# Softmax sums spread and returned by small DMAs, with one stream shuffle in place of two DVE transposes, in a sliding-window attention and GEGLU kernel

## Chip, cores and metric

The kernel runs on one NeuronCore of a Trainium2 chip. The metric is the device time of one execution in microseconds. PE is TensorE (PEld its weight loads), DVE VectorE, ACT ScalarE, POOL GpSimd, and SP the engine whose queue issues most of the DMAs. Each engine works through its own instructions in order.

## What is computed

The input x is one sequence of 2048 rows and 448 columns in bf16. The output is x plus causal attention of 16 heads (28 columns each, a window of 256 keys) plus a GEGLU feed-forward part of 1792 columns, both on the layer-normed x.

```python
qkv = (x @ wqkv) ...                                   # q, k, v: 16 heads of 28
scores = einsum("bhqd,bhkd->bhqk", q, k) * (Dh ** -0.5)
mask = (idx[:, None] - idx[None, :] >= 0) & (idx[:, None] - idx[None, :] < 256)
p = softmax(where(mask, scores, -1e9), axis=-1)
A = einsum("bhqk,bhkd->bhqd", p, v) ... @ wo
B = (gelu(x @ w_gate) * (x @ w_up)) @ w_down
return x + A(layernorm(x)) + B(layernorm(x))
```

The kernel takes the exponential without subtracting a maximum, and carries a column of ones behind the 28 columns of v (line 137), so that the product of p and v also gives the sum of p, the softmax sum, as a 29th row of each head. What the change touches is how that sum is inverted and multiplied into the product.

## The kernel before, in words

The 2048 queries are four blocks of 512 (`qb` 0 to 3, loop at line 613). Each block has an attention part (`attention`, line 445) and a feed-forward part (`gated`, line 338); the down projection of a block (`gen_down`, which also multiplies by wo) and the projections of the next (`gen_proj`) or, in the last block, `gen_up`, are cut into pieces and fed between the attention steps of the following block, by costs in ns (`Feed`, `share`, `drain`). All of this happens while the program is built; on the chip every engine has a fixed order.

The 16 heads are four groups `g` of four. A group's four heads lie in the four quarters of the partitions, 32 each: in quarter j, rows 0 to 27 are the head's columns and row 28 is its softmax sum. Blocks 1 to 3 have ten steps (`steps_of`, numbered `i` from 0). In step i, in this order:

- the masks of step i-1, three DVE products of 64-key tiles (`apply_masks`, line 432);
- `inverse()` for a group whose product is ready (line 500);
- at steps 4, 6 and 9, `pv(g)` of groups 0, 1 and 2: the products of p and v go to two PSUM banks (`ov`, line 476, for the two halves of keys), ACT copies the first to `oh` (line 482), DVE adds the second and writes `oc` (line 483);
- the score matmuls into `sc` (line 509), four PSUM banks and only one such tile, and ACT's exponential to `p_sb` (line 513);
- `scale_o()`: POOL multiplies `oc` by the inverses `rb` into `oN` (line 465), which `gen_down` reads in the next block;
- pieces of the fed work: po (lines 296, 301), pq and pk (line 218), ue (line 218), each with an eviction: `res` by DVE and its store by SP (lines 306, 307), `qT` by ACT, `kT` by DVE (266, 267), `hT` by DVE (335).

Group 3 has its `pv(3)` in `rest()` (line 539), which runs inside the first feed-forward pair (`f = 0`), followed by its inverse in `hook(0)`. Block 0 has twelve steps, its masks are done by POOL, and it has no `oh`.

`inverse()` (line 450) takes the sum out of row 28 of each quarter. DVE transposes `oc` in 32x32 blocks to `l1` (line 454), copies the sums, now 16 a partition, to `l_all` (455), takes the reciprocal (457), and transposes a broadcast of it back (459), so that `rb` holds each query's inverse in all 32 rows of its quarter. `oc` and `rb` have one buffer each; `l1` and `oh` share one.

PSUM has two banks of the tag `m`, one of `o` and one of `d`, and the four of the scores. `ov` takes both `m` banks (group 3: one `m` and one other), and so do, in turn, the fed pq, pk, pv and ue. So the matmuls that next need an `m` bank wait until `oh` (first bank) and `oc` (second bank) have read it. After the attention the four score banks become two `gt` tiles; the first up-projections `u` of `f = 0` come ahead of the first `gt`, and the first of them takes an `m` bank.

At the end DVE compares all the sums in `l_all` with two limits; a general path runs if one is outside, which does not happen with these inputs.

Of the kernel before, what the change touches and what calls it, by code (L numbers as in the profile page):

```python
# [9 lines left out]
ALU = mybir.AluOpType  # L10
AX = mybir.AxisListType
bf16 = mybir.dt.bfloat16
f32 = mybir.dt.float32
i32 = mybir.dt.int32

S, D, H, Dh, F = 2048, 448, 16, 28, 1792
P = 128
NT = S // P
NF = F // P
QB, NB = 512, 4  # L20
# [55 lines left out]
def kernel(  # L76
# [11 lines left out]
    nc = tc.nc  # L88
# [3 lines left out]
    work = fast.enter_context(tc.tile_pool(name="work", bufs=3))  # L92
# [82 lines left out]
    l_all = const.tile([P, NB * 4, 16], f32, name="l_all")  # L175
# [269 lines left out]
    def attention(qb, feeds, aux, plan):  # L445
        oN = blk.tile([P, 4, QB], bf16, name="oN")
        oNs[qb] = oN
        parts, copied, later, fresh = {}, [], [], []

        def inverse():  # L450
            while copied:
                g, oc = copied.pop(0)
                l1 = work.tile([P, 16, 32], f32, name="l1", tag="l1", bufs=1)
                nc.vector.transpose(out=l1[:, :, :].rearrange("p a b -> p (a b)"), in_=oc[:, :])
                nc.vector.tensor_copy(out=l_all[:, 4 * qb + g, :], in_=l1[:, :, Dh])
                ri = work.tile([P, 16], f32, name="ri")
                nc.vector.reciprocal(out=ri[:, :], in_=l_all[:, 4 * qb + g, :])
                rb = work.tile([P, 16, 32], f32, name="rb", bufs=1)
                nc.vector.transpose(out=rb[:, :, :], in_=ri[:, :].unsqueeze(2).to_broadcast([P, 16, 32]))  # L459
                later.append((g, oc, rb))  # L460

        def scale_o():
            while later:
                g, oc, rb = later.pop(0)
                nc.gpsimd.tensor_tensor(out=oN[:, g, :], in0=oc[:, :], in1=rb[:, :, :].rearrange("p a b -> p (a b)"), op=ALU.mult)  # L465

        def pv(g):

            tags = ("o",) if not qb else ("m", "m" if g < 3 else down_tag[0])
            ov = [psum.tile([P, QB], f32, name="ov", tag=tag, bufs=2 if tag == "m" else 1) for tag in tags]  # L470
            todo = parts.pop(g)
            for n, (half, kt, q0, nq, col, p_sb) in enumerate(todo):
                k0 = 64 * half if half else 0
                r = slice(k0, k0 + (P if half is None else 64))
                for j in range(4):
                    nc.tensor.matmul(ov[half or 0][32 * j:32 * j + 32, q0:q0 + nq], lhsT=v_sb[r, kt, 4 * g + j, :],  # L476
                                     rhs=p_sb[r, j, col:col + nq], start=n == (half or 0), stop=n + len(tags) >= len(todo),
                                     tile_position=(k0, 32 * j), skip_group_check=True)
            oc = work.tile([P, QB], f32, name="oc", bufs=1)
            if qb:  # L480
                oh = work.tile([P, QB], f32, name="oh", tag="l1", bufs=1)
                nc.scalar.copy(out=oh[:, :], in_=ov[0][:, :])  # L482
                nc.vector.tensor_tensor(out=oc[:, :], in0=oh[:, :], in1=ov[1][:, :], op=ALU.add)  # L483
            else:
                nc.vector.tensor_copy(out=oc[:, :], in_=ov[0][:, :])
            copied.append((g, oc))

        if qb:
            feeds[0].run()
        steps = list(steps_of(qb))  # L490
        pvs = {4: 0, 6: 1, 9: 2} if qb else {4: 0, 7: 1, 10: 2}
        for i, (scores, ncol, edges) in enumerate(steps):
            while (qb, scores[-1][0]) not in done:
                feeds[0].run()
            for fd in feeds:
                if fd.held:
                    fd.run()
            while fresh:
                apply_masks(*fresh.pop(0))
            inverse()  # L500
            if i in pvs:
                pv(pvs[i])
            ss = phase[0].pool.tile([P, 4, QB], f32, name="sc", tag="s")
            p_sb = work.tile([P, 4, QB], bf16, name="p_sb", bufs=5)
            for g, half, kt, q0, nq, col in scores:
                k0, nk = (64 * half, 64) if half is not None else (0, P)
                for j in range(4):
                    r = slice(32 * j, 32 * j + 32)
                    nc.tensor.matmul(ss[k0:k0 + nk, j, col:col + nq], lhsT=kT[r, g, kt * P + k0:kt * P + k0 + nk],  # L509
                                     rhs=qT[r, g, qb * QB + q0:qb * QB + q0 + nq], start=True, stop=True,  # L510
                                     tile_position=(32 * j, k0), skip_group_check=True)
                parts.setdefault(g, []).append((half, kt, q0, nq, col, p_sb))
            nc.scalar.activation(out=p_sb[:, :, 0:ncol], in_=ss[:, :, 0:ncol], func=ACT.Exp, scale=SCALE)  # L513
            if qb:
                fresh.append((p_sb, edges))
            else:
                for m in edges:
                    masked(p_sb, *m)
            scale_o()
            left = len(steps) - i  # L520
            if left == 1:
                drain(feeds)
            elif not qb:
                share(feeds + [Feed()], 1e12, 0)
            else:
                to = plan.get(i, 0)
                whole = sum(f.left for f in feeds) + STEP * left + PV * sum(j > i for j in pvs)
                ahead = STEP + PV * (i + 1 in pvs) + (360 if to > 1000 else 0)
                late = 400 if i == 0 else 0
                want = (whole - late) / (left + 0.2) + late - ahead - to  # L530
                if i in pvs:
                    had = feeds[0].left
                    share(feeds[:1], min(1100, want), 0)
                    want -= had - feeds[0].left
                share(feeds, want, to)
            if aux:
                aux.pop(0)()

        def rest():
            while fresh:  # L540
                apply_masks(*fresh.pop(0))
            after()
            pv(3)
        def after():
            inverse()
            scale_o()
        return rest, after


# [63 lines left out]
    for qb in range(NB):  # L613
        early = ()
        aux, plan = [], {}
        if qb < 2:
            aux = [lambda: rstd(6, 2), lambda: (norm(6), norm(7), loads()), lambda: None] * (1 - qb) + [lambda t=t: stat(t) for t in range(8, 12)] * (1 - qb) + [lambda: rstd(4 * qb + 8, 4)]
        if qb == 0:
            new_hT(0)
            early = (2, 8)  # L620
            feeds = [Feed((v23, 360), (gen_qk(0, (1, 2, 3)), 3 * QK1), (gen_proj(1), PROJ), (gen_up(0, early), UP1 * len(early)))]
            feeds[0].held = True
        else:
            ring[0] = ("m",)
            tags = "dodo" if last_tag[0] == "o" else "odod"
            feeds = [Feed((gen_down(qb - 1, tags), DOWN))]
            if qb < 3:
                feeds.append(Feed((gen_proj(qb + 1), PROJ)))
                plan = {0: 1140, 1: 1140, 2: 1300, 4: 1300, 6: 1300, 7: 1300}
            else:  # L630
                new_hT(3)
                early = (2, 4, 6, 8, 10)
                feeds.append(Feed((gen_up(3, early), UP1 * len(early))))
                plan = {0: 1300, 2: 1300, 4: 1300, 6: 1300, 7: 1300}
        if qb:
            score_pool(1)
        rest, after = attention(qb, feeds, aux, plan)
        nc.scalar.preload_act_table(ACT.Gelu_apprx_tanh)
        score_pool(2)
        if qb not in hTs:  # L640
            new_hT(qb)

        def hook(f):
            if f == 0:
                after()
            elif f >= 4 and qb < 2:
                t = 4 * qb + 4 + f // 2
                if f < 12:
                    norm(t + 2)
                    dma_transp(t + 2)  # L650
                    if qb == 0:
                        stat(t + 6)

        gated(qb, early, rest, hook)
        if qb < NB - 1:
            nc.scalar.preload_act_table_set("natural_log_exp_and_others")


    g1 = work.tile([P, 512], f32, name="g1", tag="l1", bufs=1)
    g2 = work.tile([P, 512], f32, name="g2", tag="rb", bufs=1)  # L660
    okc = const.tile([P, 1], f32, name="okc")
    okb = const.tile([P, 1], bf16, name="okb")
    one = const.tile([P, 1], bf16, name="one")
# [131 lines left out]
```

## Time and profile before

| | before |
|---|---|
| median of 3 runs | 235.08 us (234.16 to 235.28) |
| the profiled execution's own time | 235.08 us |
| its span in the profile | 233.3 us |
| PE busy | 216.8 us, 93% |
| DVE busy | 157.1 us, 67% |
| ACT busy | 133.4 us, 57% |
| POOL busy | 43.3 us, 19% |
| mean granted PE clock | 0.986 |

The span is what lies between the first and last instruction of the profile; 1.8 us of the execution's time lie around it. A group line gives the source line, engine and operation, output and input, count, busy time and mean of one, and the idle time of the engine ahead of it with its releaser. The chain of waits is followed back from the last instruction; it is 82% PE and 10% DVE.

### The profile page before, as it was taken

What the parts mean: (1) busy time and instruction counts of PE and PEld (TensorE: products, weight loads), DVE (VectorE), ACT (ScalarE), POOL (GpSimd) and SP (SyncE); (2) the same over time, 40 slices, a digit from 0 to 9 for tenths busy, and PEclk for the clock granted to TensorE, in tenths of its full rate; (3) what the DMA queues carried; (4) which work ended last, traced back from release to release, by engine and by line L of the source; (5) the groups of instructions that cost most, each with busy time, mean ns of one, the idle gap of its engine ahead of it and who ended that gap; (6) DMA issues with size and microseconds to landing.
All of it is one profiled execution on the core that took longest, in us unless ns stands there. A gap on an engine that the chain in (4) does not pass through costs nothing.

```text
span 233.3 us, 5303 instructions
## 1 busy us (share of the span) xinstructions
PE 216.8 (93%) x2237; PEld 97.2 (42%) x2262; DVE 157.1 (67%) x359; ACT 133.4 (57%) x129; POOL 43.3 (19%) x63
## 2 busy tenths in 40 slices
PE   6789999999999799999999799999999889999990
PEld 2433333344444344444444345444444425444470
DVE  5896877769666795755575886754456877695310
ACT  3578898435878674523778686323867737454000
POOL 8524777220000220210000220220000202220000
PEclk9999999999999999999999999999999979999997
DMA  6917999312100000012100001000000000000011
GB/s 222 301 32 78 302 288 254 125 22 49 22 22 3 20 17 25 4 22 48 22 0 22 24 3 37 5 0 0 3 21 3 22 0 22 20 3 0 21 43 27
DMA packets 15686, 12.58 MB, mean 54 GB/s; under 512 B 7401, under 2 KB 14633, under 8 KB 15657
## 3 DMA queue, kind: packets, MB, share of 16 engines
q1 hardware_dynamic: 15112, 11.38, 18.5%
q10 hardware_dynamic: 544, 0.80, 1.0%
q8 instruction: 19, 0.31, 0.6%
q14 instruction: 11, 0.08, 0.1%
HBM read 8.77 MB, written 1.84 MB: 45 GB/s over the span
## 4 chain that ended last, share of the span: by engine, by line
PE 82%; DVE 10%; DMA 3%; issue 2%; ACT 1%; SPq 0%
PE po L301 17%; PE gt L218 16%; PE u L218 12%; PE gt L223 5%; PE sc L509 5%; PE po L296 5%; PE ue L218 4%; PE pk L218 4%; PE ov L476 4%; PE pv L218 4%; PE pq L218 3%; DVE p_sb L432 3%; DMA wv<-in_A_wqkv_dram 3%; PE pq L223 2%; PE ue L223 1%
## 5 line engine op out<-in xcount | busy, mean ns | idle before, releaser
L513 ACT ACTIVATE p_sb<-sc 128x2048 bf16<-128x2048 f32 (+2 forms) x42 | 73.8, 1758 | 13.6 <-PE sc L509 12.6
L301 PE MATMUL po<-wd,hT 128*128 128x448 bf16 (+1 forms) x238 | 50.2, 343 | 0.0
L465 POOL TENSOR_TENSOR oN<-oc,rb 128x512 bf16<-128x512 f32 x16 | 21.2, 1323 | 150.8 <-DVE rb L459 150.8
L376 ACT ACTIVATE ge<-gt 128x1024 bf16<-128x1024 f32 x28 | 28.7, 1025 | 35.4 <-PE u L223 22.2
L218 PE MATMUL gt<-xnT,wg 128*128 128x512 bf16 x162 | 39.3, 380 | 0.8 <-issue 0.8
L380 DVE TENSOR_TENSOR hT<-ge,u 128x512 bf16<-128x512 bf16 x42 | 26.9, 682 | 17.1 <-ACT ge L376 16.9
L218 PE MATMUL u<-xnT,wu 128*128 128x512 bf16 x120 | 30.2, 379 | 0.3
L432 DVE TENSOR_TENSOR p_sb<-p_sb,masks 128x256 bf16<-128x256 bf16 (+1 forms) x90 | 28.7, 375 | 1.8 <-ACT p_sb L513 1.8
L301 PEld LDWEIGHTS <-hT 128*128 128x128 bf16 x238 | 21.6, 98 | 18.6 <-issue 2.2
L218 PEld LDWEIGHTS <-wu 128*128 128x128 bf16 x168 | 16.3, 99 | 21.9 <-issue 4.2
L218 PEld LDWEIGHTS <-wg 128*128 128x128 bf16 x168 | 15.1, 98 | 21.5 <-issue 5.2
L306 DVE TENSOR_TENSOR res<-po,x_sb 128x448 bf16<-128x448 f32 (+1 forms) x17 | 10.0, 590 | 15.9 <-PE po L301 15.9
L509 PE MATMUL sc<-qT,kT 32*64 32x320 bf16 (+7 forms) x640 | 16.9, 263 | 0.4 <-ACT p_sb L513 0.3
L442 POOL TENSOR_SCALAR_AFFINE_SELECT p_sb<-p_sb 128x512 bf16<-128x512 bf16 (+1 forms) x20 | 14.2, 727 | 13.4 <-ACT p_sb L513 13.4
L296 PE MATMUL po<-wo,oN 128*128 128x448 bf16 (+1 forms) x68 | 16.3, 343 | 0.0
L267 DVE CAST kT<-pk 128x512 bf16<-128x512 f32 (+1 forms) x17 | 10.9, 644 | 7.9 <-PE pk L223 7.9
L218 PE MATMUL pk<-xnT,wkp 128*128 128x512 bf16 (+1 forms) x51 | 13.1, 366 | 3.2 <-DVE oc L483 3.1
L482 ACT COPY oh<-ov 128x512 f32<-128x512 f32 x12 | 7.0, 586 | 15.1 <-PE ov L476 13.0
L266 ACT CAST qT<-pq 128x512 bf16<-128x512 f32 (+1 forms) x17 | 9.5, 559 | 9.9 <-PE pk L223 9.9
L335 DVE CAST hT<-ue 128x512 bf16<-128x512 f32 x14 | 9.0, 687 | 8.2 <-PE ue L223 8.2
L218 PE MATMUL ue<-xnT,wu 128*128 128x512 bf16 x38 | 11.7, 420 | 2.2 <-DVE oc L483 1.8
L223 PE MATMUL gt<-xnT,wgu 64*128 64x512 bf16 x49 | 13.6, 379 | 0.0
(70 smaller groups left out, 228.6 us busy)
## 6 DMA issues: line engine op xcount, KB each, us to landing
out_dram<-res SPq DMA_DIRECT2D x15, 112.0 KB, 1.7
wd<-in_B_w_down_dram SPq DMA_DIRECT2D x1, 1568.0 KB, 12.0
wu<-in_B_w_up_dram SPq DMA_DIRECT2D x1, 1344.0 KB
wg<-in_B_w_gate_dram SPq DMA_DIRECT2D x1, 1344.0 KB, 13.6
x_sb<-in_A_x_dram SPq DMA_DIRECT2D x1, 896.0 KB, 7.1
wraw<-in_A_wqkv_dram ACTq DMA_DIRECT2D x1, 672.0 KB, 5.4
x_sb<-in_A_x_dram SPq DMA_DIRECT2D x1, 448.0 KB, 4.7
wo<-in_A_wo_dram SPq DMA_DIRECT2D x4, 98.0 KB
```

What stands on the lines that cost most here:

```text
L218: nc.tensor.matmul(ps, lhsT=lhs(c), rhs=rhs(c), start=start and c == 0, stop=stop and c == 2, skip_group_check=True)
L223: nc.tensor.matmul(ps, lhsT=lhs[p0:p0 + 64], rhs=rhs[p0:p0 + 64], start=start, stop=stop, tile_position=(p0, 0), skip_group_check=True)
L267: nc.vector.tensor_copy(out=kT[:, g, ts], in_=pk[:, 0:n])
L296: nc.tensor.matmul(po[:, 0:w], lhsT=oN[:, g, cs], rhs=wo[:, g, lo:up], start=(g == 0), stop=False, skip_group_check=True)
L301: nc.tensor.matmul(po[:, 0:w], lhsT=hT[:, f, cs], rhs=wd[:, f, lo:up], start=False, stop=(f == NF - 1), skip_group_check=True)
L376: nc.scalar.activation(out=ge[:, :, :], in_=pr["gt"][:, :, :], func=ACT.Gelu_apprx_tanh)
L380: nc.vector.tensor_tensor(out=hT[:, f + i, :], in0=ge[:, i, :], in1=u[:, :], op=ALU.mult)
L432: nc.vector.tensor_tensor(out=reg, in0=reg, in1=m, op=ALU.mult)
L442: nc.gpsimd.affine_select(out=reg, in_=reg, pattern=mid + [[1 if diag else -1, min(w, P)]], compare_op=ALU.is_ge, fill=0.0, base=0 if diag ...
L465: nc.gpsimd.tensor_tensor(out=oN[:, g, :], in0=oc[:, :], in1=rb[:, :, :].rearrange("p a b -> p (a b)"), op=ALU.mult)
L509: nc.tensor.matmul(ss[k0:k0 + nk, j, col:col + nq], lhsT=kT[r, g, kt * P + k0:kt * P + k0 + nk], rhs=qT[r, g, qb * QB + q0:qb * QB + q0 + ...
L513: nc.scalar.activation(out=p_sb[:, :, 0:ncol], in_=ss[:, :, 0:ncol], func=ACT.Exp, scale=SCALE)
```

## The change

In blocks 1 to 3 `inverse()` is replaced by three functions. `spread` issues four DMAs from SP right after `oc` is written: each takes one quarter's sum row (512 values in one partition) and writes it as 16 values into each of the 32 partitions of the quarter in `l_all`. `back` takes the reciprocal on DVE and issues four DMAs that write the inverses back as one row of `oc`, row 29 of each quarter, which is not otherwise used. `spread_rows` is one DVE stream shuffle that copies row 29 of each quarter to all 32 rows, giving `rb`. `back` runs in steps 5 and 7 (groups 0 and 1, behind the exponential), in `rest()` (group 2, ahead of `pv(3)`) and in `hook(2)` (group 3); `spread_rows` runs ahead of `pv` in steps 7 and 9, in `hook(0)` and in `hook(4)`.

The buffers change too: `oc` alternates between two (`wa`, `wb`), and `oh` and the shuffled `rb` share one (`wc`). Block 0 keeps the two transposes, one group at a time. The DVE masks are the same in both, and in both they come first in each step.

```diff
-        def inverse():
-            while copied:
-                g, oc = copied.pop(0)
-                l1 = work.tile([P, 16, 32], f32, name="l1", tag="l1", bufs=1)
-                nc.vector.transpose(out=l1[:, :, :].rearrange("p a b -> p (a b)"), in_=oc[:, :])
-                nc.vector.tensor_copy(out=l_all[:, 4 * qb + g, :], in_=l1[:, :, Dh])
-                ri = work.tile([P, 16], f32, name="ri")
-                nc.vector.reciprocal(out=ri[:, :], in_=l_all[:, 4 * qb + g, :])
-                rb = work.tile([P, 16, 32], f32, name="rb", bufs=1)
-                nc.vector.transpose(out=rb[:, :, :], in_=ri[:, :].unsqueeze(2).to_broadcast([P, 16, 32]))
-                later.append((g, oc, rb))
+        def inverse(g, oc):
...
+        def spread(g, oc):
+            for j in range(4):
+                nc.sync.dma_start(out=l_all[32 * j:32 * j + 32, 4 * qb + g, :],
+                                  in_=oc[32 * j + Dh:32 * j + Dh + 1, :].rearrange("p (a b) -> p a b", b=16))
+        def back():
+            g, oc = copied[0]
+            ri = work.tile([P, 16], f32, name="ri")
+            nc.vector.reciprocal(out=ri[:, :], in_=l_all[:, 4 * qb + g, :])
+            for j in range(4):
+                nc.sync.dma_start(out=oc[32 * j + Dh + 1:32 * j + Dh + 2, :].rearrange("p (a b) -> p a b", b=16),
+                                  in_=ri[32 * j:32 * j + 32, :])
+        def spread_rows():
+            g, oc = copied.pop(0)
+            rb = work.tile([P, QB], f32, name="rb", tag="wc", bufs=1)
+            nc.vector.stream_shuffle(out=rb[:, :], in_=oc[:, :], mask=[Dh + 1] * 32)
+            later.append((g, oc, rb))
...
-            oc = work.tile([P, QB], f32, name="oc", bufs=1)
+            oc = work.tile([P, QB], f32, name="oc", tag="wb" if qb and g % 2 else "wa", bufs=1)
             if qb:
-                oh = work.tile([P, QB], f32, name="oh", tag="l1", bufs=1)
+                oh = work.tile([P, QB], f32, name="oh", tag="wc", bufs=1)
                 nc.scalar.copy(out=oh[:, :], in_=ov[0][:, :])
                 nc.vector.tensor_tensor(out=oc[:, :], in0=oh[:, :], in1=ov[1][:, :], op=ALU.add)
...
             copied.append((g, oc))
+            if qb:
+                spread(g, oc)
...
             while fresh:
                 apply_masks(*fresh.pop(0))
-            inverse()
+            if not qb and copied:
+                inverse(*copied.pop(0))
+            if qb and i in (7, 9):
+                spread_rows()
             if i in pvs:
                 pv(pvs[i])
...
             scale_o()
+            if qb and i in (5, 7):
+                back()
...
         def rest():
             while fresh:
                 apply_masks(*fresh.pop(0))
-            after()
+            if qb:
+                back()
             pv(3)
-        def after():
-            inverse()
-            scale_o()
+        def after(f):
+            if f == 0:
+                if qb:
+                    spread_rows()
+                else:
+                    inverse(*copied.pop(0))
+                scale_o()
+            elif qb and f == 2:
+                back()
+            elif qb and f == 4:
+                spread_rows()
+                scale_o()
...
         def hook(f):
-            if f == 0:
-                after()
-            elif f >= 4 and qb < 2:
+            after(f)
+            if f >= 4 and qb < 2:
```

More of the change, by code (lines that the diff above doesn't have):

```diff
@@ L448, in attention @@
         parts, copied, later, fresh = {}, [], [], []
-        def inverse():
-            while copied:
-                g, oc = copied.pop(0)
-                l1 = work.tile([P, 16, 32], f32, name="l1", tag="l1", bufs=1)
-                nc.vector.transpose(out=l1[:, :, :].rearrange("p a b -> p (a b)"), in_=oc[:, :])
-                nc.vector.tensor_copy(out=l_all[:, 4 * qb + g, :], in_=l1[:, :, Dh])
-                ri = work.tile([P, 16], f32, name="ri")
-                nc.vector.reciprocal(out=ri[:, :], in_=l_all[:, 4 * qb + g, :])
-                rb = work.tile([P, 16, 32], f32, name="rb", bufs=1)
-                nc.vector.transpose(out=rb[:, :, :], in_=ri[:, :].unsqueeze(2).to_broadcast([P, 16, 32]))
-                later.append((g, oc, rb))
+        def inverse(g, oc):
+            l1 = work.tile([P, 16, 32], f32, name="l1", tag="wc", bufs=1)
+            nc.vector.transpose(out=l1[:, :, :].rearrange("p a b -> p (a b)"), in_=oc[:, :])
+            nc.vector.tensor_copy(out=l_all[:, g, :], in_=l1[:, :, Dh])
+            ri = work.tile([P, 16], f32, name="ri")
+            nc.vector.reciprocal(out=ri[:, :], in_=l_all[:, g, :])
+            rb = work.tile([P, QB], f32, name="rb", tag="wb", bufs=1)
+            nc.vector.transpose(out=rb[:, :].rearrange("p (a b) -> p a b", b=32), in_=ri[:, :].unsqueeze(2).to_broadcast([P, 16, 32]))
+            later.append((g, oc, rb))
[5 more added lines that the diff above has]
+            g, oc = copied[0]
+            ri = work.tile([P, 16], f32, name="ri")
+            nc.vector.reciprocal(out=ri[:, :], in_=l_all[:, 4 * qb + g, :])
[6 more added lines that the diff above has]
+            nc.vector.stream_shuffle(out=rb[:, :], in_=oc[:, :], mask=[Dh + 1] * 32)
+            later.append((g, oc, rb))
         def scale_o():
@@ L464, in scale_o @@
                 g, oc, rb = later.pop(0)
-                nc.gpsimd.tensor_tensor(out=oN[:, g, :], in0=oc[:, :], in1=rb[:, :, :].rearrange("p a b -> p (a b)"), op=ALU.mult)
+                nc.gpsimd.tensor_tensor(out=oN[:, g, :], in0=oc[:, :], in1=rb[:, :], op=ALU.mult)
         def pv(g):
@@ L656 @@
             nc.scalar.preload_act_table_set("natural_log_exp_and_others")
-    g1 = work.tile([P, 512], f32, name="g1", tag="l1", bufs=1)
-    g2 = work.tile([P, 512], f32, name="g2", tag="rb", bufs=1)
+    g1 = work.tile([P, 512], f32, name="g1", tag="wc", bufs=1)
+    g2 = work.tile([P, 512], f32, name="g2", tag="wb", bufs=1)
     okc = const.tile([P, 1], f32, name="okc")
```

## The prediction

> **What bounds the kernel now.** I read the page first, then PE's waits, then the timeline around each of them, then the same stretch of every engine one step later.
>
> ```profile
> PE 216.8 (93%) x2237; PEld 97.2 (42%) x2262; DVE 157.1 (67%) x359; ACT 133.4 (57%) x129; POOL 43.3 (19%) x63
> ```
>
> PE is the bound: 16.5 us of the span are not PE's, and the DMA loads at the start and the last store take most of that. DVE at 67% is no bound on average, so work taken from it is worth only what PE waits for DVE. PE's waits say where that is:
>
> ```profile
> PE pk L218 <- DVE oc L483: 3.1, 2, 1.6
> PE ue L218 <- DVE oc L483: 1.8, 1, 1.8
> PE sc L509 <- ACT p_sb L513: 0.3, 1, 0.3
> ```
>
> Three waits, 1.53, 1.62 and 1.84 us, one in each of blocks 1 to 3: 4.99 us in all. PE wants an `m` bank that `oc` of group 1 has not yet read. No other wait in mid-kernel is over 0.3 us. The timeline of block 1 at this place:
>
> ```profile
> 73.32 0.69 DVE L267 CAST kT<-pk 128x512 bf16<-128x512 f32 x1 [1.51 <-PE pk L223]
> 73.93 0.82 DVE L432 TENSOR_TENSOR p_sb<-p_sb,masks 128x256 bf16<-128x256 bf16 x3
> 74.66 0.71 DVE L454 STREAM_TRANSPOSE l<-oc 128x512 f32<-128x512 f32 x1
> 75.41 0.18 DVE L455 COPY l_all<-l 128x16 f32<-128x16 f32 x1
> 75.62 0.25 DVE L457 RECIPROCAL ri<-l_all 128x16 f32<-128x16 f32 x1
> 75.90 0.71 DVE L459 STREAM_TRANSPOSE rb<-ri 128x512 f32<-128x512 f32 x1
> 76.54 0.58 DVE L306 TENSOR_TENSOR res<-po,x_sb 128x448 bf16<-128x448 f32 x1
> 76.69 1.27 POOL L465 TENSOR_TENSOR oN<-oc,rb 128x512 bf16<-128x512 f32 x1 [28.44 <-DVE rb L459]
> 77.05 1.60 DVE L432 TENSOR_TENSOR p_sb<-p_sb,masks 128x256 bf16<-128x256 bf16 x3
> 78.57 0.67 DVE L483 TENSOR_TENSOR oc<-oh,ov 128x512 f32<-128x512 f32 x1
> 79.30 0.81 PE L218 MATMUL pk<-xnT,wkp 128*128 128x512 bf16 x3 [1.53 <-DVE oc L483]
> ```
>
> See two things: the inverse of group 0 (74.66 to 76.61) stands ahead of everything `oc` waits for, and the three masks behind it take 1.60 us while POOL scales, against 0.82 just before. PE had been ready since 77.77. The second place is step 9, where nothing waits today:
>
> ```profile
> 85.54 0.75 PE L476 MATMUL ov<-p_sb,v_sb 64*32 64x320 bf16 x48
> 86.37 0.59 ACT L482 COPY oh<-ov 128x512 f32<-128x512 f32 x1 [0.71 <-ACT p_sb L513]
> 86.86 1.88 ACT L513 ACTIVATE p_sb<-sc 128x2048 bf16<-128x2048 f32 x1
> 89.62 1.46 PE L218 MATMUL u<-xnT,wu 128*128 128x512 bf16 x5
> 90.92 1.46 PE L218 MATMUL gt<-xnT,wg 128*128 128x512 bf16 x6
> ```
>
> `u` takes the bank that `oh` reads, `gt` the banks that the exponential reads. Counted from the start P of `pv(2)`, they start at P+4.08 and P+5.38; today `oh` ends at P+1.42 and the exponential at P+3.20.
>
> **What the skill says.** "VectorE: DVE Perf Modes", the perf-mode tier table: a stream shuffle has only a one-element-per-cycle program, and one-rate operations fit (N+151)/0.96 ns. For 512 elements that is an estimate of 0.69 us; the two transposes here took 0.705 and 0.711, which agrees. "SBUF — State Buffer", Who interferes with whom: a DVE instruction with two SBUF inputs and a GpSimd instruction that reads SBUF block each other. The 1.60 against 0.82 us agrees. "DMA: Bandwidth & Descriptors", Anatomy of one DMA: a DMA has a fixed cost of about 2.0 us whatever its size, most of it the receipt of the last write, heaviest for HBM. No SBUF-to-SBUF copy is in this trace; stores to HBM land after 1.7, so 64-byte rows need not be cheaper:
>
> ```profile
> L307 SPq DMA_DIRECT2D out_dram<-res x17: 332/332/382, 68.1 to 228.3; - x17
> DMA to landing us min/median/max: 1.5/1.7/3.1
> ```
>
> **The change part by part.**
>
> *PE, ACT and the masks* keep their instructions and order in both programs; only waits differ.
>
> *Removed*: 12 times two transposes and a copy, 705+175+711 = 1.59 us, 19.1 us of DVE. *Added*: 12 shuffles of 0.69, 8.3 us. DVE gets 10.8 us back; only what stands ahead of the three waits counts. Bounds of the shuffle: 0.6 to 1.0 us; at 1.0, 0.3 more at step 9.
>
> *The DMA round trip T* is the main unknown: SP issues four in a row, 0.33 us each with 0.05 between, so the fourth starts at +1.14 and lands 1.7 later; with 0.1 for semaphores T = 2.95 us. Ends: 2.65 with a landing of 1.5; 5.0 with issues of 0.6 (the slow loads at the start) and a landing of 3.1. Below that only a faster issue could go, which gains nothing: the slack below covers it. SP has 96 more issues, over 32 us, but waits 137 us for `res` in total; its order per block is spread 0, back 0, store, spread 1, back 1, store, spread 2, store, back 2, spread 3, back 3, so a store can wait for a back but is not on PE's path.
>
> *Step 5 and 6, block 1.* `oc` of group 0 ends at 71.81; its sums are back at 74.76. The reciprocal waits for them on DVE; behind it are queued `res`, the masks of step 5 and `oc` of group 1. The masks ahead of it end at 74.75, so it waits for nothing: 75.0. Then `res` (its po is done by about 74.7) to 75.65, the masks, with POOL idle, to 76.5 (exponential done 75.65), and `oc`, whose `oh` ends at 76.65, to 77.35. PE needs it at 77.77. The whole wait goes, with 0.4 us to spare (T may reach 3.5). What is next late is the exponential of step 6, done 78.43 where the next scores want the banks at 78.84. Block 2 has the same pattern 54.1 us later. Block 3: `oc` 0 ends 179.80, sums back 182.75, before the masks end at 183.3; `oh` at about 184.5, `oc` at 185.2, needed at 185.75. Gain 1.53+1.62+1.84 = 4.99.
>
> *Step 7.* Masks, shuffle of group 0 (80.5 to 81.2), POOL, reciprocal of group 1 at 81.2; its sums were back at 80.3, its inverses return at 84.4. Nothing late.
>
> *Step 9, the new wait.* The masks of step 8, then the shuffle of group 1 to `wc`, then POOL's scaling, then `oh` of group 2, which overwrites `wc` and so waits for POOL. Behind `oh` on ACT stands the exponential of step 9; behind them `u` and `gt`. Block 1, from P (84.0 now): `res` -0.3 to 0.3, masks to 1.14 (inverses at 0.4, in time), shuffle to 1.84, POOL 1.27 to 3.17, `oh` 3.2 to 3.8, exponential to 5.6. `u` at 4.08 is spared; `gt` wanted 5.38: 0.3 us lost. Block 2 the same. In block 3 the masks of step 8 end at P+1.42, and `u` and `gt` come at P+3.70 and P+4.99: shuffle to 2.1, POOL to 3.5, `oh` to 4.1, exponential to 5.9. `u` loses 0.45 and `gt` 0.5 more: 0.95.
>
> *Group 2 and 3.* The reciprocal of group 2 waits for its DMAs ahead of `oc` of group 3: block 1, `oc` 2 at P+4.5, back at P+7.5, and `oc` 3 comes at about P+9: covered. The old wait of `oc` 3 for POOL (1.39 us each) goes, but `hT` behind it waits for ACT anyway. The shuffle of group 3 waits on DVE about 1.3 us in `hook(4)`; behind it are the norms for a later block, and in block 3 three `hT` products that then run 1 to 2 us late. `ge` has two buffers and PE is at most held by the third after it, so I cost this at nothing; without that cover up to 1 us. Taking DVE's contention with POOL out of step 6 puts it to step 7, where a cast from PSUM runs.
>
> *Sum*: -4.99+0.3+0.3+0.95 = -3.4. The profiled execution took 235.08, its span 233.3 and 1.8 around it, and equals the median of the runs: 235.08-3.4 = 231.7.
>
> **The rivals.** (1) *The new wait doesn't show*: if `gt` or `u` come later than I think or POOL starts sooner, all 4.99 stay: 230.1. For it: the step-9 margins are tenths. Against: `oh` is behind POOL in any case. (2) *The DMA path takes the transposes' place.* `back` and `spread` are read by an engine in order, and `spread_rows` of group 1 sits ahead of `oh`, the exponential and two PSUM banks. Above T = 3.5 each us of T gives back a us at step 6 of blocks 1 and 2; above the same 3.5 the inverses of group 1, two round trips later, are late at step 9, by 2 us for each us. Blocks 1 and 2 break even at about 3.9, the whole at about 4.1. At T = 4.5 blocks 1 and 2 lose 1.7 each (1.0 at step 6 and 0.3+2.0 at step 9, less 1.6), block 3 loses 0.3, together 3.7: 238.8. For it: four issues in a row and 64-byte rows; the slowest store landed after 3.1. Against: the median of 1.7 and an idle DMA system in these stretches. (3) *In between*, T of 3.7 to 4.3, gains and losses cancel: about 235.
>
> **How the numbers follow.** Forecast 0.56, rival 1 0.17, rival 2 0.14, rival 3 0.13. A measurement of this kernel can tell about 0.5%, 1.2 us, from no change. The range reaches from rival 1 (230.1) to a T of about 3.9, where only block 3 still gains (234.3); what is left out is most of rival 2 and half of rival 3. Faster by over 0.5% 0.74, within 0.11, slower 0.15.
>
> **What would show it.** PE's waits for `oc` gone from pk and ue; in step 6 masks at 0.82 us again. In step 9 ACT's `oh` waiting for POOL by about 2 us, and PE's `gt` (in block 3 also `u`) waiting for ACT by 0.3 to 0.9. Spread to landing of the fourth near 2.9 us. Wrong if the reciprocals wait long for DMA, if a shuffle takes over 1 us, or if PE waits for `ge` in block 3.

## The result and the profile after

The changed kernel is slower: 243.3 us median of 4 runs (242.89 to 244.7) against 234.68 us (234.16 to 235.28, 4 runs), a ratio of 1.0377 with a 95% interval of 1.0325 to 1.0429. The profiled execution took 242.89 us with a span of 241.0 us, 7.7 us more than before's 233.3. Ratios, here and below, leave out runs over 1.5% above the fastest of the same kernel, which are two of the 20 of one kernel below.

The line of the engines and the chain of waits, by engine, from the page of the changed kernel:

```profile
PE 220.6 (92%) x2237; PEld 97.9 (41%) x2262; DVE 143.2 (59%) x347; ACT 133.3 (55%) x129; POOL 43.6 (18%) x63
PE 57%; DVE 12%; DMA 10%; SPq 8%; ACT 6%; issue 3%; POOL 2%; DVEq 0%; POOLq 0%; ACTq 0%
```

DVE did lose work, 157.1 to 143.2 us. But the chain, 82% PE before, is only 57% PE now, and runs for 18% of the span through DMA transfers and SP's queue; before these had 3%, the load of a weight at the start. The waits of the changed kernel (engine, line, what it waited for: us in total, times, longest):

```profile
DVE ri L470 <- DMA l_all<-oc: 17.1, 12, 2.4
DVE rb L478 <- DMA oc<-ri: 16.4, 9, 3.2
ACT oh L501 <- POOL oN L484: 17.2, 3, 6.4
PE u L218 <- ACT oh L501: 6.1, 3, 2.7
PE pk L218 <- DVE oc L502: 0.9, 1, 0.9
PE po L296 <- POOL oN L484: 0.7, 1, 0.7
PE gt L223 <- ACT ge L376: 0.7, 1, 0.7
PE gt L218 <- ACT p_sb L537: 0.7, 2, 0.3
```

Read it from the top: all 12 reciprocals and 9 of 12 shuffles wait for their DMAs on DVE; three `oh`, one a block, wait for POOL on ACT; and PE's `u` waits for `oh`. The old waits for `oc` shrank from 4.99 to 0.9 us, so step 6 went nearly as forecast. The loss is one step of the chain further on. Block 1, the stretch that the prediction worked out:

```profile
71.25 0.69 DVE L502 TENSOR_TENSOR oc<-oh,ov 128x512 f32<-128x512 f32 x1
71.96 2.52 SPq L464 DMA_DIRECT2D l_all<-oc  x4
76.69 0.25 DVE L470 RECIPROCAL ri<-l_all 128x16 f32<-128x16 f32 x1 [1.82 <-DMA l_all<-oc]
77.01 2.45 SPq L472 DMA_DIRECT2D oc<-ri  x4
78.07 0.68 DVE L502 TENSOR_TENSOR oc<-oh,ov 128x512 f32<-128x512 f32 x1
78.80 0.81 PE L218 MATMUL pk<-xnT,wkp 128*128 128x512 bf16 x3 [0.91 <-DVE oc L502]
79.56 0.53 SPq L307 DMA_DIRECT2D out_dram<-res  x1
80.19 2.43 SPq L464 DMA_DIRECT2D l_all<-oc  x4
83.93 0.25 DVE L470 RECIPROCAL ri<-l_all 128x16 f32<-128x16 f32 x1 [1.85 <-DMA l_all<-oc]
84.21 2.44 SPq L472 DMA_DIRECT2D oc<-ri  x4
85.05 0.75 PE L495 MATMUL ov<-p_sb,v_sb 64*32 64x320 bf16 x48
87.93 0.73 DVE L478 STREAM_SHUFFLE rb<-oc 128x512 f32<-128x512 f32 x1
88.73 1.26 POOL L484 TENSOR_TENSOR oN<-oc,rb 128x512 bf16<-128x512 f32 x1 [5.31 <-DVE rb L478]
90.03 0.58 ACT L501 COPY oh<-ov 128x512 f32<-128x512 f32 x1 [4.87 <-POOL oN L484]
90.67 1.46 PE L218 MATMUL u<-xnT,wu 128*128 128x512 bf16 x5 [1.37 <-ACT oh L501]
92.45 1.46 PE L218 MATMUL gt<-xnT,wg 128*128 128x512 bf16 x6 [0.33 <-ACT p_sb L537]
```

Three things are to be seen. A burst of four issues keeps SP busy for 2.43 to 2.52 us in these lines, where 1.47 was forecast. `oc` of group 1 is complete at 78.75, but its spread starts at 80.19: SP is still issuing group 0's return (77.01 to 79.46) and then a store. And from the spread at 80.19 two ways follow one another, the sums out and the inverses back: 3.74 us to the reciprocal, and 3.70 from the return's first issue to the mask load (87.91) that comes with the shuffle, so that the inverses are there 2.86 us after `pv(2)` started, where the prediction had them 0.4 after. Shuffle, POOL, `oh` and `u` then stand in a row.

Where PE's order stands against before, by the start of the same instruction in both traces:

| PE instruction | before | after | later by |
|---|---|---|---|
| first `pv`, block 1 | 69.67 | 69.79 | 0.12 |
| `pk` behind `oc` of group 1, block 1 | 79.30 | 78.80 | -0.50 |
| first `gt`, block 1 | 90.92 | 92.45 | 1.53 |
| first po of block 2 | 112.30 | 114.37 | 2.07 |
| `pk` behind `oc` of group 1, block 2 | 133.42 | 133.83 | 0.41 |
| first `u`, block 2 | 143.75 | 146.74 | 2.99 |
| first po of block 3 | 166.42 | 171.16 | 4.74 |
| `ue` behind `oc` of group 1, block 3 | 187.59 | 190.32 | 2.73 |
| first `sc` behind the halved clock of before, block 3 | 192.74 | 193.94 | 1.20 |
| first `gt`, block 3 | 199.71 | 205.16 | 5.45 |
| first po of block 3's own output | 213.81 | 219.96 | 6.15 |
| last po | 226.33 | 233.69 | 7.36 |

Three falls are a step 6 (0.62, 1.66 and 2.01 us gained); most rises are a step 9 or the tail of a block. The rest is PE's clock, which was halved for 3.4 us in both traces: after at about 148 us, in block 2 (from 2.99 to 4.74), and before at about 190 us, in block 3 (from 2.73 to 1.20). That costs 1.75 and 1.53 us, so all but 0.2 cancels by the end.

### The profile page after: what moved, and what is told of

It reads as the page before. It is cut to its first block, busy times and chain, and to the rows that moved or that the text cites. A ratio compares the mean times of both kernels' runs of the same rounds, so it can differ in the third digit from the quotient of the medians.

```text
span 241.0 us, 5474 instructions
## 1 busy us (share of the span) xinstructions
PE 220.6 (92%) x2237; PEld 97.9 (41%) x2262; DVE 143.2 (59%) x347; ACT 133.3 (55%) x129; POOL 43.6 (18%) x63
## 4 chain that ended last, share of the span: by engine, by line
PE 57%; DVE 12%; DMA 10%; SPq 8%; ACT 6%; issue 3%; POOL 2%; DVEq 0%; POOLq 0%; ACTq 0%
PE gt L218 10%; PE po L301 10%; PE u L218 8%; DMA oc<-ri 5%; DMA l_all<-oc 5%; SPq L464 4%; SPq L472 4%; PE gt L223 3%; PE sc L533 3%; PE po L296 3%; PE ov L495 3%; PE pv L218 3%; PE pk L218 3%; PE pq L218 3%; PE ue L218 2%
## 5 line engine op out<-in xcount | busy, mean ns | idle before, releaser
L218 PE MATMUL gt<-xnT,wg 128*128 128x512 bf16 x162 | 40.6, 389 | 1.5 <-issue 0.8
L432 DVE TENSOR_TENSOR p_sb<-p_sb,masks 128x256 bf16<-128x256 bf16 (+1 forms) x90 | 24.6, 329 | 3.5 <-ACT p_sb L537 3.5
L502 DVE TENSOR_TENSOR oc<-oh,ov 128x512 f32<-128x512 f32 x12 | 8.3, 688 | 9.7 <-ACT oh L501 9.5
```

What stands on the lines that cost most here:

```text
L218: nc.tensor.matmul(ps, lhsT=lhs(c), rhs=rhs(c), start=start and c == 0, stop=stop and c == 2, skip_group_check=True)
L432: nc.vector.tensor_tensor(out=reg, in0=reg, in1=m, op=ALU.mult)
```

## The experiments

Theory A: the time is lost on the DMA path. Each way is four issues in a row on SP, at 0.6 us each, and a landing behind the last; a second group's spread queues behind the first one's return; an engine in order (DVE) waits for it, and the shared buffer and the tail hand the wait on to PE. Its rivals: that the DMAs themselves slow the other engines, by traffic or by SP's work, whoever waits for them; that the transfer of such small rows, not the issue, is what takes long; that the shared buffer `wc` alone costs it. All ratios are against the kernel before, run beside on the same chip.

**The shared buffer.** In the changed kernel, ACT's copy goes straight to `oc`, and DVE adds in place, so that nothing on ACT waits for POOL.

```diff
-                oh = work.tile([P, QB], f32, name="oh", tag="wc", bufs=1)
-                nc.scalar.copy(out=oh[:, :], in_=ov[0][:, :])
-                nc.vector.tensor_tensor(out=oc[:, :], in0=oh[:, :], in1=ov[1][:, :], op=ALU.add)
+                nc.scalar.copy(out=oc[:, :], in_=ov[0][:, :])
+                nc.vector.tensor_tensor(out=oc[:, :], in0=oc[:, :], in1=ov[1][:, :], op=ALU.add)
```

> ACT writes its copy of the first half straight into oc and DVE adds in place, so that nothing of group 2 shares a buffer with the shuffled inverses of group 1. Theory A (the inverses of group 1 return about 3 us late, and the shared buffer passes this on to the copy, the exponential of step 9, u and gt): PE's waits of step 9, 6.1 us for the copy and 0.7 us for the exponential, go, though the shuffle stays as late as it is; the time falls from 243.3 to about 236.5. Rival B (the DVE waits for the DMAs in the feed-forward part, groups 2 and 3, cost most): little changes, above 241.

Measured: 236.13 us (234.67 to 238.39, 20 runs), ratio 1.0086 (1.0062 to 1.0111). PE's waits in its profiled execution, which at 238.39 us is the longest of the 20:

```profile
PE gt L218 <- ACT ge L376: 2.4, 1, 2.4
PE ov L495 <- DVE kT L267: 1.6, 1, 1.6
PE ov L495 <- DVE hT L335: 1.2, 2, 1.0
PE pk L218 <- DVE oc L501: 1.0, 1, 1.0
PE po L296 <- POOL oN L484: 0.7, 1, 0.7
```

The wait of `u` is gone and some 7 us with it. But DVE still waits for DMAs, 20.7 us ahead of its reciprocals in this trace, and what stands behind a wait on DVE (`kT`, `hT`, and through `hT` and `ge` the `gt` of PE) now reaches PE. The buffer carries the wait; it is not its source.

**Half the DMAs.** Only the sums of two quarters go there and back. The other two heads of each group are multiplied by row 29 of `oc` as `pv` leaves it, which is zero, so in blocks 1 to 3 this kernel leaves half of the heads out; the instructions on the engines stay, but for one memset that gives the unused sums a value.

```diff
-            for j in range(4):
+            for j in range(2):
                 nc.sync.dma_start(out=l_all[32 * j:32 * j + 32, 4 * qb + g, :],
...
-            for j in range(4):
+            for j in range(2):
                 nc.sync.dma_start(out=oc[32 * j + Dh + 1:32 * j + Dh + 2, :].rearrange("p (a b) -> p a b", b=16),
```

> Only quarters 0 and 1 are spread and sent back (two DMAs each way instead of four); the heads of quarters 2 and 3 are left out of the attention, their output is zero. Everything else stays, the shared buffer too. Theory A (what is late is the queue of issues of 0.62 us on SP): each round trip is 1.25 us shorter and the wait of group 1's spread behind group 0's return on SP goes; group 1's inverses are back before the shuffle wants them, PE's wait for oc at step 6 goes, its waits at step 9 fall to the forecast 0.3, 0.3 and 0.95 us; 232 to 234. Rival C (the shared buffer costs this much whenever the shuffle is, or the landing of 64-byte rows is what is slow): 239 or more.

Measured: 229.71 us (228.93 to 232.1), ratio 0.982 (0.9743 to 0.9897), with `oh` still in the shared buffer; under the 232 to 234 expected. PE's waits:

```profile
PE gt L219 <- ACT p_sb L538: 0.7, 2, 0.3
PE u L219 <- ACT oh L502: 0.5, 1, 0.5
```

With a short burst no wait for `oc` is left, and step 9 costs what the prediction worked out or less: `gt` waits 0.33 us in block 1 (forecast 0.3), nothing waits in block 2 (forecast 0.3), and in block 3 `u` waits 0.48 and `gt` 0.33 (forecast 0.45 and 0.5).

**One DMA in place of four, all of the bytes.** Is it the number of issues or the transfer of 64-byte rows? One DMA reads the four rows (a partition step of 32) and writes all 128 partitions; the return likewise. The whole computation is there.

```diff
-            for j in range(4):
-                nc.sync.dma_start(out=l_all[32 * j:32 * j + 32, 4 * qb + g, :],
-                                  in_=oc[32 * j + Dh:32 * j + Dh + 1, :].rearrange("p (a b) -> p a b", b=16))
+            nc.sync.dma_start(out=l_all[:, 4 * qb + g, :], in_=oc[Dh::32, :].rearrange("p (a b) -> p a b", b=16))
...
-            for j in range(4):
-                nc.sync.dma_start(out=oc[32 * j + Dh + 1:32 * j + Dh + 2, :].rearrange("p (a b) -> p a b", b=16),
-                                  in_=ri[32 * j:32 * j + 32, :])
+            nc.sync.dma_start(out=oc[Dh + 1::32, :].rearrange("p (a b) -> p a b", b=16), in_=ri[:, :])
```

> The changed kernel with one DMA in place of four each way: one spread carries the four sum rows (4 partitions of 512 values to 128 partitions of 16), one back carries the four rows of inverses; all bytes and all heads stay, oh and rb still share wc. If the number of issues sets the round trip (theory A: 0.6 us of SP each, and the queue behind them), the round trip of a group falls from 3.7 to 4.7 us to about 2.5 (one issue of 0.6, one landing of 1.7, 0.1 to 0.2 for semaphores), group 1's spread no longer queues behind a long return, and the time is that of the kernel with two quarters, 229 to 231 us. If the rows of 64 bytes set it, so that one DMA of 128 rows takes as long to issue or to land as four of 32, the round trip stays near 4 us and the time near 240 to 243.

Measured: 229.1 us (228.53 to 230.21), ratio 0.9787 (0.9764 to 0.981). Block 1 again:

```profile
71.90 0.67 SPq L463 DMA_DIRECT2D l_all<-oc  x1
74.72 0.24 DVE L468 RECIPROCAL ri<-l_all 128x16 f32<-128x16 f32 x1
75.04 0.58 SPq L469 DMA_DIRECT2D oc<-ri  x1
76.78 0.69 DVE L498 TENSOR_TENSOR oc<-oh,ov 128x512 f32<-128x512 f32 x1 [0.21 <-ACT oh L497]
77.50 0.56 SPq L463 DMA_DIRECT2D l_all<-oc  x1
81.10 0.55 SPq L469 DMA_DIRECT2D oc<-ri  x1
84.93 0.72 DVE L474 STREAM_SHUFFLE rb<-oc 128x512 f32<-128x512 f32 x1
```

None of these waits for a DMA, and the spread of group 1 follows its `oc` at once. Where a shuffle did wait in this kernel, in block 3's tail, a whole way can be read: a return issued at 201.30, shuffle at 203.20, 1.90 us, against 3.70 for four. The Trainium skill, "DMA: Bandwidth & Descriptors", Anatomy of one DMA, puts a fixed cost of about 2.0 us on a DMA. It measured that for DMAs issued by GpSimd, while these come from SP; one way of one DMA agrees with it all the same. What that price doesn't hold is the issuing of the three ahead of it. This settles two rivals: the bytes and rows are the same and the shared buffer is still there, only the number of DMAs fell, and the 14 us between this kernel and the changed one go with it. One thing else fell with it, the number of landings to be waited for, from four a way to one; the two queues below keep all 96.

**One DMA, and the copy to `oc`**: both edits above together.

> The one-DMA kernel with ACT's copy written to oc instead of oh, so that nothing on ACT waits for POOL's scaling. Theory A: the step-9 waits that are left at a short round trip (0.3, 0.3 and about 0.8 us) go too: 1 to 1.5 us less than the one-DMA kernel, 228 to 229.5 us. If rows of 64 bytes set the round trip: about 236, as with four DMAs.

Measured: 228.15 us (227.47 to 228.34), ratio 0.9736 (0.9716 to 0.9755). No wait of PE over 0.3 us is left in mid-kernel.

**Two queues.** The copy goes to `oc` as in the first experiment, and the DMAs of quarters 2 and 3 are issued by POOL, both ways.

```diff
-                nc.sync.dma_start(out=l_all[32 * j:32 * j + 32, 4 * qb + g, :],
+                (nc.sync, nc.gpsimd)[j // 2].dma_start(out=l_all[32 * j:32 * j + 32, 4 * qb + g, :],
...
-                nc.sync.dma_start(out=oc[32 * j + Dh + 1:32 * j + Dh + 2, :].rearrange("p (a b) -> p a b", b=16),
+                (nc.sync, nc.gpsimd)[j // 2].dma_start(out=oc[32 * j + Dh + 1:32 * j + Dh + 2, :].rearrange("p (a b) -> p a b", b=16),
```

> As the run with the copy written into oc (236.1), and the DMAs of quarters 2 and 3 are issued by POOL, those of 0 and 1 by SP, both ways. Theory A with POOL's issue as fast as SP's: the round trip is 1.25 us shorter, as in the run with two DMAs; 231 to 233. If POOL's issue takes 1 us or more each, or its queue stands behind the scaling: no gain or a loss, 236 to 242.

Measured: 229.16 us (228.67 to 229.77), ratio 0.9789 (0.9767 to 0.9811), better than expected: 7 us less than the same kernel on one queue (the first experiment). "Trainium Kernel Development and Optimization", Key Constraints, says that issuing from several engines only saves the sequencer's issue time. That is what it did here, and the issue time was what counted:

```profile
71.99 1.25 SPq L464 DMA_DIRECT2D l_all<-oc  x2
72.27 1.16 POOL L464 DMA_DIRECT2D l_all<-oc  x2 [23.87 <-DVE oc L501]
74.82 0.24 DVE L470 RECIPROCAL ri<-l_all 128x16 f32<-128x16 f32 x1
```

Two issues a queue, and the reciprocal comes 2.83 us after the first without a wait, where one queue had 4.73 for this group and 3.74 for the next. All 96 DMAs are there, and single landings of up to 3.8 us too, so it was not the number of landings that cost the 7 us.

**The return on POOL's queue** takes only the queueing of group 1's spread away: in the changed kernel `back` issues from POOL, four in a row as before.

```diff
-                nc.sync.dma_start(out=oc[32 * j + Dh + 1:32 * j + Dh + 2, :].rearrange("p (a b) -> p a b", b=16),
+                nc.gpsimd.dma_start(out=oc[32 * j + Dh + 1:32 * j + Dh + 2, :].rearrange("p (a b) -> p a b", b=16),
```

> The changed kernel (243.3) with the inverses sent back by POOL's queue, so that the spread of group 1 no longer stands 1.4 us behind the return of group 0 on SP. Theory A with POOL's issue as fast as SP's: group 1's inverses come 1.4 us earlier, PE's waits at step 9 fall by 1.4 in each block and the ones behind SP in the tail a little; 238 to 240. If POOL issues slower: 243 or more.

Measured: 239.43 us (238.02 to 240.66), ratio 1.0225 (1.0182 to 1.0267). In block 1:

```profile
78.04 0.68 DVE L502 TENSOR_TENSOR oc<-oh,ov 128x512 f32<-128x512 f32 x1
78.75 2.41 SPq L464 DMA_DIRECT2D l_all<-oc  x4
82.13 1.26 POOL L484 TENSOR_TENSOR oN<-oc,rb 128x512 bf16<-128x512 f32 x1 [2.46 <-DVE rb L478]
82.40 0.26 DVE L470 RECIPROCAL ri<-l_all 128x16 f32<-128x16 f32 x1 [0.36 <-DMA l_all<-oc]
83.33 2.00 POOL L472 DMA_DIRECT2D oc<-ri  x4
```

The spread of group 1 starts right behind `oc`, 1.44 us earlier than in the changed kernel. But the return now queues behind POOL's scaling and loses 0.7 of it. The queue on SP was a part, worth 3.6 us by the ratios and 3.9 by the medians; with fewer issues to a queue (one DMA, or two queues) the loss went altogether, so the burst of four is the larger part.

**The tail.** The first experiment, with groups 2 and 3 of blocks 1 to 3 back on the two transposes at their old places (`rest` and `hook(0)`). The function `inverse` is fitted to these blocks (the place in `l_all`, and `rb` in the shared buffer), which the cut leaves out.

```diff
-            if qb:
+            if qb and g < 2:
                 spread(g, oc)
...
             if qb:
-                back()
+                inverse(*copied.pop(0))
+                scale_o()
             pv(3)
...
             if f == 0:
-                if qb:
-                    spread_rows()
-                else:
-                    inverse(*copied.pop(0))
-                scale_o()
-            elif qb and f == 2:
-                back()
-            elif qb and f == 4:
-                spread_rows()
+                inverse(*copied.pop(0))
                 scale_o()
```

> As the run with the copy written into oc, and groups 2 and 3 take the two transposes of before, at their places of before; only groups 0 and 1 use DMAs. Theory A: what the tail costs shows as the difference to that run: the norms and products behind group 3's shuffle in block 1 (0.5 us) and the products, u and oN behind it in block 3 (about 2 us), together 2 to 3 us less, about 234. Rival B: this takes most of the loss, 4 us or more less than that run. If the tail is covered, no difference.

Measured: 232.42 us (230.65 to 233.15), ratio 0.99 (0.9866 to 0.9934), 3.7 us less by the medians than with the DMAs there, and 4.4 by the ratios: more than the 2 to 3 expected, and about the 4 named for rival B, though not most of the loss, which is 8.6 us. The waits of `gt` for `ge` and of po for POOL are gone from PE's list. So the tail was not free.

**A step later.** The same, and the DMAs of groups 0 and 1 are read later: `back` in steps 6 and 8, the shuffles ahead of `pv` in step 8 and behind it in step 9. Four issues on one queue stay.

```diff
-            if qb and i in (7, 9):
+            if qb and i == 8:
                 spread_rows()
...
                 pv(pvs[i])
+            if qb and i == 9:
+                spread_rows()
...
-            if qb and i in (5, 7):
+            if qb and i in (6, 8):
                 back()
```

> From the run with transposes for groups 2 and 3 (232.4): what groups 0 and 1 get back by DMA is read one step later (reciprocals at the end of steps 6 and 8, shuffles at the start of step 8 and behind oc in step 9); all four DMAs each way stay. Theory A (a round trip of 3.7 to 4.8 us is harmless where an in-order engine reads it later than that): PE's waits for oc (1.6 us) and for the casts and masks behind the reciprocals (1.6 us) go; 228.5 to 229.5. If the DMAs cost by themselves, through SP or the memory: 231 or more.

Measured: 230.21 us (229.71 to 231.16), ratio 0.9838 (0.9812 to 0.9864), somewhat over what was expected. DVE still waits for DMAs at six shuffles, 6.0 us in all, but no PE wait over 0.5 us follows from it: the same slow ways cost little where nobody needs their end. The kernel is 1.7 us over the next one, which has no DMA of sums.

**No DMA of sums at all, only the place.** From the kernel before: group 0's inverse moves from step 5 to step 7, group 1's to step 8, with the two `oc` buffers that this needs and the copy to `oc`, which were not tried alone. The transposes stay in all twelve inverses.

```diff
-            while copied:
+            if copied:
...
-            oc = work.tile([P, QB], f32, name="oc", bufs=1)
+            oc = work.tile([P, QB], f32, name="oc", tag="oc1" if g % 2 else "oc0", bufs=1)
...
-            inverse()
+            if not qb or i in (7, 8):
+                inverse()
```

> The kernel before without any DMA of sums: transposes as before, but group 0's inverse is put from step 5 to step 7 and group 1's from step 7 to step 8, oc has two buffers, ACT's copy goes into oc, the two transposes share one buffer. If the three waits for oc came from the place of group 0's inverse on DVE and not from the transposes' cost, they go: 5.0 us under before, about 230. If the masks or something else behind is late anyway: 233 or more.

Measured: 228.55 us (228.09 to 229.2), ratio 0.9753 (0.9705 to 0.9802). PE waits no more:

```profile
75.38 0.83 DVE L432 TENSOR_TENSOR p_sb<-p_sb,masks 128x256 bf16<-128x256 bf16 x3 [0.17 <-ACT p_sb L513]
76.39 0.69 DVE L482 TENSOR_TENSOR oc<-oc,ov 128x512 f32<-128x512 f32 x1 [0.18 <-ACT oc L481]
77.30 0.81 PE L218 MATMUL pk<-xnT,wkp 128*128 128x512 bf16 x3
```

`oc` of group 1 is done at 77.08, and `pk` starts 2.0 us earlier than before. DVE is as busy as before, 157.2 us; the version with one DMA and the copy to `oc` has 144.1, and its time is the same within both intervals. The 13 us of DVE work were worth nothing that can be measured; where they stood was worth 5 to 6 us.

**Unread DMAs.** The same with eight more DMAs of the sum rows behind each `oc`, written to a tile that nobody reads.

```diff
+            if qb:
+                for n in range(2):
+                    for j in range(4):
+                        nc.sync.dma_start(out=dead[32 * j:32 * j + 32, 2 * (g % 2) + n, :],
+                                          in_=oc[32 * j + Dh:32 * j + Dh + 1, :].rearrange("p (a b) -> p a b", b=16))
```

> The run with the late transposes (228.55) and, behind each oc of blocks 1 to 3, eight DMAs of a sum row to a tile that nobody reads: as many issues on SP and bytes as in the changed kernel, without its waits. Theory A (only the waits of engines for what returns cost): no change, 228 to 229.2. If the issues or the traffic cost (stores behind them on SP, res behind the stores): 230 or more.

Measured: 229.45 us (228.82 to 229.67), ratio 0.9796 (0.9775 to 0.9817), 0.4% over the kernel without them, with intervals that overlap, and between the two outcomes that were named. 96 issues, as many as in the changed kernel, cost about 1 us when no one waits for them, and by the far ends of the two intervals no more than 2.6. The rival that the DMAs by themselves slow the engines can explain no more than that of the 14 us between the changed kernel and the one with one DMA.

## Why the prediction was wrong

*What held.* The bound (PE, and only what it waits for), the place of the gain and its size: by the table some 4.3 of the forecast 4.99 us came at step 6. The shuffle: 0.728 us against the estimate of 0.69, and a mask load of 0.014 with each. ("VectorE: DVE Perf Modes" has the shuffle's tier in the perf-mode tier table; the fit stands in its section on the TRN2 errata, for an fp32 add, and came out 5% low here.) The chain of step 9, shuffle, POOL, `oh`, `u` and `gt`, in that order. With half the DMAs or one of them step 9 costs 1.1 and 0.8 us of waits where 1.55 was forecast, and the kernel is faster than the forecast 231.7. The second rival, the DMA path in place of the transposes, is what happened, at 0.14. Two of the three signs of being wrong came: the reciprocals waited for DMAs, and PE for `ge` in block 3.

*The step that failed* is the one of "the DMA round trip T", put at 2.95 us. SP's issues and landings of the changed kernel:

```profile
L464 SPq DMA_DIRECT2D l_all<-oc x48: 532/582/1225, 72.0 to 213.0; - x48
DMA to landing us min/median/max: 1.7/1.7/3.1
```

The landing was right, 1.7 us in the median. The issue was taken from lone stores (0.332 us); a copy of the burst takes 0.58 behind another one, with 0.04 between. Three such and a landing are 1.86+1.7 = 3.56, with 0.1 to 0.2 for semaphores the 3.7 us of the trace. That 0.6 stood in the prediction, as the upper end ("the slow loads at the start"), and the prediction gives no reason for the lower price. It is not the standing in a row that makes one issue dear: the first copy of a burst takes 0.54, and so does a single copy in the kernel with one DMA, whose lone stores still take 0.34. The store was the wrong kind of DMA to take the price from.

That mis-sized term alone would have been survivable: by the prediction's own rules T = 3.74 is just under its break-even of 3.9. Two more steps failed on top of it.

- *Late landings.* Group 0's sums took 4.73 us in block 1: the fourth DMA landed 2.6 after its issue. In block 3 the return of group 1 took 5.0 (195.61 to 200.63). The maximum of 3.1 was in the prediction's bounds, but as an end of the range, and not as one of many chances: with four DMAs a way, 96 in all, nine of the 50 whose landing is known took over 2.2 us. The late ones don't come at random: in five kernels (this one, the first experiment, the tail, the step later, the return on POOL's queue) it is the same two, the third and fourth DMA of block 1's first spread, at 2.6 to 3.4 us. A 16 KB packet of queue 8, which the page lists as `instruction` (by that name the loading of the program itself), runs on the core's DMA engines just then, from 74.32 to 75.29. The DMAs of the changed kernel from 73.0 to 76.6:

```profile
q8 instruction: 1, 0.02, 1.7%
l_all<-oc SPq DMA_DIRECT2D x3, 2.0 KB, 2.8
```

By the packets of its trace, all nine late landings, and all six issues of a copy that took over 0.7 us, fall on such a load of 16 or 8 KB; of the 50, the 33 that met no load in their first 1.75 us took 1.66 to 1.79. They coincide in time; no experiment here tests that the one causes the other.

- *SP's order.* The prediction wrote it out, "spread 0, back 0, store, spread 1", and asked only whether a store can wait for a back. It did not ask what spread 1 waits for, and counted group 1's way from the end of its `oc`. With bursts of 2.45 us the spread waited 1.44. The lateness of group 1's inverses in block 1, 87.91 in place of 84.4, is the sum: `oc` 1.40 later (78.75 for 77.35), the queue 1.44, two longer ways 0.79+0.75, less 0.9 that the reciprocal had to spare, together 3.5.

At step 9 this gives 1.37, 2.08 and 2.69 us for `u` and a further 0.33 twice for `gt`, together 6.8 where 1.55 was forecast.

*"I cost this at nothing"* of groups 2 and 3 failed too. Its doubt was the third `gt` after the shuffle; here are block 3's shuffle of group 3 and what it delays:

```profile
216.82 0.37 PE L223 MATMUL gt<-xnT,wgu 64*128 64x512 bf16 x1 [0.67 <-ACT ge L376]
218.89 0.01 DVE L478 LOAD_MASK_SELECT rb<-oc  x1 [3.23 <-DMA oc<-ri]
219.72 1.61 POOL L484 TENSOR_TENSOR oN<-oc,rb 128x512 bf16<-128x512 f32 x1 [5.55 <-DVE rb L478]
221.38 0.36 PE L296 MATMUL po<-wo,oN 128*128 128x448 bf16 x1 [0.69 <-POOL oN L484]
```

DVE stands 3.23 us where 1.3 were forecast, PE waits for `ge`, and then for the scaled group itself, which the prediction had not looked at: in the last block po follows at once. By the table the tails cost 0.54 us in block 1 and 1.91 in block 3; the tail experiment, from a kernel whose trace has a wait of 2.4 for `ge`, gives 3.7.

*The sum.* PE has the same 2237 instructions in the same order in both traces, so their starts can be compared one by one, and the table adds up. -4.29 at step 6; +8.86 around step 9 (6.8 of it the waits of `u` and `gt`; 1.0 at the `ov` ahead of them, of which 0.44 is a wait behind `hT` in block 3; and 1.0 by which the matmuls behind a wait start later still); +2.45 in the tails; +0.22 from the clock; and 0.12 that was there before block 1. That is the 7.36 us by which the last po is later. The forecast had -4.99 and +1.55, and nothing for the rest.

*What stays open*: whether it is the loading of instructions that makes landings late, and why the first experiment's runs spread over 3.7 us; a way of 5.9 us in its trace (80.29 to 86.19) makes late landings a likely reason, but no run shows it.

## What to carry to other kernels

Price a burst of DMAs as a row on its issuing queue, not as one latency: the issue of each one ahead, then the landing of the last, then whatever else that queue holds between two steps of the same chain; and where the shape allows, make it one DMA. When a profile shows one engine waiting behind another's work, ask first whether the work can stand later, since moving two inverses a block by one or two steps gave here all that removing 13 us of DVE work did. Before an in-order engine is made to wait for a DMA, list what is queued behind the waiting instruction, up to the end of the last block.

## What the runs showed of the hardware

- One SBUF-to-SBUF DMA between four rows of 2 KB and 128 partitions of 64 bytes (8 KB) took SP 0.54 to 0.67 us to issue. The return took 1.90 us from issue to its reader where it was waited for; the spread never was. One of 2 KB took nearly the same issue, 0.54 first in a burst and 0.58 behind another, so the number of rows didn't show in it.
- A store behind a burst of such copies took 0.53 us to issue, behind one copy 0.41 to 0.43, and a lone one 0.33 to 0.39. POOL issued the copies in 0.50 each, no slower than SP.
- Small copies landed in 1.66 to 1.79 us where no instruction load ran beside them, and in up to 3.07 where one did (the changed kernel's trace).
